# Attention's order of issue made anew in an attention and experts kernel on one core

## The chip, the core and the metric

One core of one Trainium2 chip runs the whole program. The metric is the device time of an execution in microseconds (us). Lower is better. The engines are named as the profile names them: PE (TensorE's matmuls), PEld (its weight loads), DVE (VectorE), ACT (ScalarE), POOL (GpSimd) and SP (SyncE, which issues most of the transfers).

## The reference

Three layers follow each other. The change touches only the first and the first preparation of the second.

```python
# attention: batch 4, 8 heads, 576 positions, 64 per head
scores = scale * np.matmul(q, k.transpose(0, 1, 3, 2))
cum = np.cumsum(np.log(np.clip(f, 0.0001, 1.0)), axis=-1)
scores = np.where(causal, -1000000000.0, scores + cum[:, :, :, None] - cum[:, :, None, :])
attn = np.exp(scores - np.max(scores, axis=-1, keepdims=True))
attn = attn / (np.sum(attn, axis=-1, keepdims=True) + 1e-09)
x = np.matmul(attn, v)            # then laid out as 2304 tokens of 512
# gated layer, widths 512 to 1024 to 512
x = (((x @ w1) * (x @ w2)) @ w3) @ w_out
# experts: each token goes to one of 8, widths 512 to 1024 to 512
y[t] = gate_w[t] * eom[t] * (np.maximum(x[t] @ e1[e], 0) @ e2[e])
```

## The kernel before

**Attention's tiles.** A pair of heads fills the 128 partitions, 64 for each head, so there are 16 pairs (4 batches of 4). The scores are wanted more exactly than one matmul in `fp32r` gives. So q and k are split: the high part is a copy by ACT (`high`, L191, stages `qh` and `kh`), the low part is the rest, by DVE (`low`, L198, `ql` and `kl`). A second set of scores, from the high parts alone, serves to find each row's maximum.

**The stages of a pair.** `lk`, `lq`, `lv` load (L176). `ck` puts the decays into `CK` (L183, L185): for pair 0 from the tile `EK`, for the others from its copy in DRAM, `EKd` (L188). `qd` moves the last 64 queries on the diagonal of `QD` (L171). `X0` to `X3` are the scores for the maxima (L205), and `m0` to `m3` the maxima (L231, two instructions each, one per head). `XL` (L223, L224) and `mL` (L231 on `xl`) do the last 64 rows, which stand alone. `Tm` turns the maxima `M` by a matmul with the identity (L238), `tc` copies them (L241), and `mv` sends them on SP (L171) to `MR`, one row for each head. `GA` to `GD` are the exact scores of four banks (L205, three products each), and `HA` to `HD` add decay and maximum (L205 with `MR` and `CK`). `eA` to `eD` are the exponentials by ACT (L267). `a0` to `a4` cut off the later keys on POOL (L273, "select"), `s1` to `s3` add the blocks on POOL for the row sums (L285). `p0`, `p1`, `p3` multiply with v (L294), `su` sums (L310), `xa` and `sa` copy the results out (L314, L317), and `zs` stores the sums (L321). For each batch, `ri` (L329 to L332) loads its sums, adds 1e-9, inverts them on DVE and stores them to `rz`. `xl` and `xm` (L69, L340), in pairs 7 and 11 alone, load inverses and multiply the first tokens with them on POOL. `cr` clears rows for the experts (L350).

**Weights in between.** `w3` and `w_out` are multiplied with each other once, exactly, before the gated layer uses them. They come as 24 pieces of 64-bit numbers. `Combined.narrow` takes a piece through seven steps: `c0` the load (L430), `c1` ACT (L437), `c2`, `c3`, `c4` on DVE (L439, L441, L443), `c5` ACT (L446) and `c6` POOL (L448). Three buffers hold loaded pieces, and `c4` is the last to read one; four hold the pieces in work. `EARLY` = 12 pieces are done within attention, one in each pair from the third on. The 16 products (`product`, L494 to L496, 12 matmuls each) come after it, the first four of them (`P0` to `P3`) beside the last pair, and the other pieces are converted beside the products.

**What sets the order.** Each engine runs its instructions in the order in which they are issued. Within attention a table sets that order: stage x of pair n has the time `START[x] + PERIOD * n`, all are sorted by it, and they are issued in that order. `AFTER` adds entries behind the last pair. The times in the table are labels to sort by.

```python
order = [(START[x] + SHIFT.get((n, x), 0.0) + PERIOD * n, n, i, x) for n in range(B * NP) for i, x in enumerate(START)]
order = sorted(order + [(t + PERIOD * (B * NP - 1), B * NP, 0, x) for x, t in AFTER.items()])
```

Of the kernel before, what the change touches and what calls it, by code (L numbers as in the profile page):

```python
# [28 lines left out]
P = 128  # L29
# [32 lines left out]
    "inputs": 14.0, "scores": 14.6, "P0": 28.2, "P1": 28.3, "P2": 30.3, "P3": 30.4,  # L62
# [9 lines left out]
def attention(nc, tc, ident, xT, rz, xs, wc, q, k, v, f):  # L72
# [7 lines left out]
    with (  # L80
# [32 lines left out]
        Ms = [p1.tile([P, 32], F32, name=f"M{i}") for i in range(2)]  # L113
# [64 lines left out]
        def decay(s):  # L178
            n = s["n"]
            for h in range(2):  # L180
                dst = CKs[n % 3][64 * h + 1:64 * h + 3, :S]
                if n == 0:
                    move(dst, EK[h:h + NH + 1:NH])  # L183
                else:
                    SP.dma_start(out=dst.bitcast(F32), in_=EKd[:, 2 * n + h, :])  # L185
            if n == 0:
# [50 lines left out]
        def turn(s):  # L237
            PE.matmul(s["x", 4][0:32, 896:1024], Ms[s["n"] % 2], ident, start=True, stop=True)  # L238
# [84 lines left out]
        def invert(s):  # L323

            if s["n"] % NP == NP - 1:
# [3 lines left out]
                SP.dma_start(out=z, in_=view(zd))  # L329
                V.tensor_scalar(out=z, in0=z, scalar1=1e-9, scalar2=None, op0=ALU.add)  # L330
                V.reciprocal(z, z)
                SP.dma_start(out=view(rz), in_=z)  # L332
# [9 lines left out]
        def clear_rows(s):  # L342
# [12 lines left out]
            "zs": (store_sums,), "ri": (invert,), "cr": (clear_rows,), "xl": (first_tile, 0), "xm": (first_tile, 1),  # L355
# [11 lines left out]
        for step in range(7):  # L367
            stages[f"c{step}"] = (lambda s, step: wc.upto(step, min(s["n"] - 1, EARLY)), step)
# [856 lines left out]
```

## Time and profile before

| | |
|---|---|
| time, median of 3 runs | 864.07 us (863.25 to 866.69) |
| the profiled execution's own time | 864.87 us |
| its span, first to last instruction | 863.3 us |
| mean granted clock of TensorE, as a share of full speed | 0.972 |
| PE busy | 804.7 us (93%) |
| DVE busy | 458.8 us (53%) |
| POOL busy | 373.4 us (43%) |
| ACT busy | 280.3 us (32%) |

Attention takes about the first quarter of the span. The shares are means over the whole of it, and over the 40 slices of the page they change much:

```profile
PE   6898898998969889999999999998899999999995
PEld 3666566666747668788788788897778899999983
DVE  6589879780798862333234033044456845446430
ACT  2456456552355441221221221222122122232321
POOL 5477689695365572013023021014255544354421
PEclk7799999899989999999999999999999999999998
DMA  3446675601555311001010010034556564566460
```

Each digit is a slice of 21.6 us (863.3 / 40), in tenths of it, and a 9 is 90% or more. The first ten slices are attention, the next two or three the products of the weights. The last line but one is the clock granted to TensorE. In a timeline row stand the start, the duration, the engine, the line, the operation, out <- in by the program's names and the shapes; in brackets, where the engine had been idle, for how long and what ended that.

### The profile page before, as it was taken

The numbers are of one execution on the slowest core, as the hardware profiler recorded it, in microseconds if no ns is written. First come the engines' busy times: TensorE is split into PE (matmuls) and PEld (weight loads), VectorE is DVE, ScalarE is ACT, GpSimd is POOL, SyncE is SP. The second block draws the span as 40 slices with busy tenths as digits, with TensorE's granted clock in tenths as the row PEclk, the third lists the DMA queues.
The fourth block names the chain that finished last, engine by engine and source line by source line (L and its number), as shares of the span: only waits on it lengthen the run. The fifth ranks groups of instructions, "written<-read, shape, count | busy, mean of one in ns | idle before, by whom it ended". The sixth has DMA issues, their size and how long they took to land.

```text
span 863.3 us, 13769 instructions
## 1 busy us (share of the span) xinstructions
PE 804.7 (93%) x5140; PEld 652.2 (76%) x5140; DVE 458.8 (53%) x950; ACT 280.3 (32%) x536; POOL 373.4 (43%) x383
## 2 busy tenths in 40 slices
PE   6898898998969889999999999998899999999995
PEld 3666566666747668788788788897778899999983
DVE  6589879780798862333234033044456845446430
ACT  2456456552355441221221221222122122232321
POOL 5477689695365572013023021014255544354421
PEclk7799999899989999999999999999999999999998
DMA  3446675601555311001010010034556564566460
GB/s 97 121 132 207 188 226 170 184 22 37 194 170 182 137 49 39 25 38 36 13 50 19 0 44 13 1 106 139 157 149 232 192 207 132 185 204 207 147 254 28
DMA packets 40340, 102.12 MB, mean 118 GB/s; under 512 B 8610, under 2 KB 9314, under 8 KB 40016
## 3 DMA queue, kind: packets, MB, share of 16 engines
q1 hardware_dynamic: 37088, 91.46, 33.5%
q0 software_dynamic: 3184, 9.77, 3.0%
q8 instruction: 41, 0.67, 0.3%
q14 instruction: 27, 0.22, 0.1%
HBM read 84.49 MB, written 16.51 MB: 117 GB/s over the span
## 4 chain that ended last, share of the span: by engine, by line
PE 63%; DVE 14%; DMA 10%; issue 8%; ACT 2%; POOL 1%; SPq 0%; POOLq 0%; DVEq 0%; ACTq 0%
DVE junk L231 4%; PE y L532 4%; PE y L531 4%; PE y L530 4%; DMA xs<-xr,pos 3%; PE h L532 3%; PE h L530 3%; PE h L531 3%; PE a L530 3%; PE a L532 3%; PE b L530 3%; PE a L531 3%; PE b L531 3%; PE b L532 3%; PE v L294 2%
## 5 line engine op out<-in xcount | busy, mean ns | idle before, releaser
L560 DVE TENSOR_TENSOR ga<-b,ga 128x512 f32<-128x512 f32 (+1 forms) x40 | 25.4, 636 | 150.4 <-PE b L532 147.3
L675 POOL DMA_INDIRECT xs<-xr,pos x18 | 19.1, 1062 | 186.0 <-DVE pos L671 130.6
L231 DVE CUSTOM_DVE_ANT_0 junk<-x,tri 128x256 f32<-128x256 f32 (+3 forms) x128 | 62.7, 490 | 9.9 <-PE x L205 0.8
L530 PE MATMUL h<-gh,ah 128*128 128x320 f32 (+4 forms) x224 | 67.2, 300 | 0.0
L531 PE MATMUL h<-gl,ah 128*128 128x320 f32 (+4 forms) x224 | 66.9, 299 | 0.0
L532 PE MATMUL h<-gh,al 128*128 128x320 f32 (+4 forms) x224 | 66.9, 299 | 0.0
L530 PE MATMUL a<-xh,w1h 128*128 128x512 f32 (+1 forms) x160 | 60.9, 381 | 3.2 <-ACT w1h L446 2.2
L532 PE MATMUL a<-xh,w1l 128*128 128x512 f32 (+1 forms) x160 | 60.0, 375 | 3.2 <-POOL w1l L448 3.2
L530 PE MATMUL b<-xh,w2h 128*128 128x512 f32 (+1 forms) x160 | 60.5, 378 | 0.9 <-DVE raw L735 0.9
L273 POOL TENSOR_SCALAR_AFFINE_SELECT PT<-PT 128x256 f32<-128x256 f32 (+1 forms) x80 | 40.3, 522 | 47.4 <-ACT PT L267 47.4
L531 PE MATMUL b<-xl,w2h 128*128 128x512 f32 (+1 forms) x160 | 59.9, 374 | 0.0
L531 PE MATMUL a<-xl,w1h 128*128 128x512 f32 (+1 forms) x160 | 59.9, 374 | 0.0
L532 PE MATMUL b<-xh,w2l 128*128 128x512 f32 (+1 forms) x160 | 59.4, 372 | 0.0
L530 PE MATMUL y<-raw,gh 128*128 128x512 f32 x144 | 57.7, 401 | 1.4 <-ACT gh L561 1.4
L532 PE MATMUL y<-raw,gl 128*128 128x512 f32 x144 | 56.8, 394 | 0.9 <-DVE gl L563 0.9
L531 PE MATMUL y<-raw,gh 128*128 128x512 f32 x144 | 57.0, 396 | 0.0
L523 POOL TENSOR_SCALAR bh<-rb 128x1024 fp32r<-128x1024 f32 x28 | 34.8, 1245 | 48.1 <-DMA rb<-e 40.8
L561 ACT ACTIVATE gh<-ga 128x512 fp32r<-128x512 f32 (+1 forms) x40 | 23.6, 590 | 95.9 <-DVE ga L560 95.9
L951 DVE SCALAR_TENSOR_TENSOR hl<-h,hh 128x320 fp32r<-128x320 f32 (+4 forms) x56 | 25.4, 463 | 50.6 <-ACT hh L950 49.8
L294 PE MATMUL v<-PT,vr 128*64 128x448 f32 (+4 forms) x384 | 49.8, 396 | 1.1 <-ACT zs L317 1.1
L285 POOL TENSOR_TENSOR ac<-ac,PT 128x640 f32<-128x640 f32 (+1 forms) x32 | 44.5, 1390 | 2.6
L524 DVE TENSOR_TENSOR bl<-rb,bh 128x1024 fp32r<-128x1024 f32 x28 | 37.8, 1373 | 14.1 <-POOL bh L523 14.1
(610 smaller groups left out, 2230.0 us busy)
## 6 DMA issues: line engine op xcount, KB each, us to landing
ra<-e SPq DMA_DIRECT2D x28, 512.0 KB
rb<-e SPq DMA_DIRECT2D x28, 512.0 KB
w<-w3t SPq DMA_DIRECT2D x16, 512.0 KB
xs<-zero SPq DMA_DIRECT2D x8, 771.0 KB
vr<-v SPq DMA_DIRECT2D x16, 320.0 KB
kr<-k SPq DMA_DIRECT2D x16, 288.0 KB
qr<-q SPq DMA_DIRECT2D x16, 288.0 KB
wo<-wo SPq DMA_DIRECT2D x8, 512.0 KB
```

The costliest lines, as they stand in the source:

```text
L231: V.tensor_tensor_reduce(out=junk[:, :w], in0=s["x", i][:, 512 * h:512 * h + w] if i < 4 else s["x", i][:, 224:224 + S], in1=tri[:, 640 - ...
L273: G.affine_select(out=t, in_=t, pattern=[[0, 2], [1, w]], compare_op=ALU.is_ge, fill=0.0, base=0, channel_multiplier=-1,)
L285: G.tensor_tensor(out=acc[:, :, q0 - P:], in0=first if j == 1 else acc[:, :, q0 - P:], in1=src, op=ALU.add)
L294: PE.matmul(s["v"][HALF[h], 384 + q0:384 + q1], s["vr"][:, j, HALF[h]], place(s, j, h, q0, q1), start=(j == 0), stop=(j == 4 or q1 == P),)
L523: G.tensor_scalar(out=hi, in0=src, scalar1=1.0, scalar2=1.0, op0=ALU.mult, op1=ALU.mult)
L524: lo_eng.tensor_tensor(out=lo, in0=src, in1=hi.bitcast(F32), op=ALU.subtract)
L530: PE.matmul(ps, ah, bh, start=start and i == 0, stop=False)
L531: PE.matmul(ps, ah, bl, start=False, stop=False)
L532: PE.matmul(ps, al, bh, start=False, stop=stop and i == last)
L560: V.tensor_tensor(out=ga[:, :w], in0=pb[:, :w], in1=ga[:, :w], op=ALU.mult)
L561: A.activation(out=gh[:, f, :w], in_=ga[:, :w], func=ACTF.Copy)
L951: V.scalar_tensor_tensor(out=hl[:, f, :w], in0=ps[:, :w], scalar=0.0, in1=hh[:, f, :w].bitcast(F32), op0=ALU.max, op1=ALU.subtract)
```

## The change

The table `START` has a new time for nearly every stage, so the order of issue changes on every engine. `AFTER` gets ten entries of a new kind: `Kx_y` brings step x of the weights' conversion to y pieces done. With these and with `EARLY + 2` for the first two steps, four pieces more (12 to 15) are through DVE's steps within the last pairs, and loads of more are issued. The inversion of a batch's sums becomes three stages: `rl` the load, `rv` DVE's step, 21.4 later in the table, and `rs` the store. The maxima have 64 instead of 32 columns, and the turn fills 64 partitions. The decays of pairs 0, 1 and 2 come straight from `EK`, and the copy to DRAM is made with pair 2's. The arithmetic is the same.

```diff
 PERIOD = 9.8
 START = {
...
-    "kl": -4.4, "m1": -3.17, "m3": -3.16, "m2": -2.79, "c0": -2.74, "X0": -2.67, "m0": -2.37, "ql": -1.52, "qd": 0.69,
...
+    "kl": 1.21, "XL": 2.1, "mL": 3.54, "Tm": 3.61, "tc": 3.98, "ql": 4.35, "mv": 6.59, "cr": 7.59, "GA": 8.35,
...
 AFTER = {
-    "inputs": 14.0, "scores": 14.6, "P0": 28.2, "P1": 28.3, "P2": 30.3, "P3": 30.4,
+    "K4_13": 3.595, "K0_15": 3.605, "K0_16": 3.615, "K4_14": 3.625, "K0_17": 3.635, "inputs": 11.329, "scores": 13.382,
+    "K1_15": 18.064, "K1_16": 18.074, "K4_15": 18.084, "K0_18": 18.094, "K4_16": 18.104, "P0": 28.286, "P1": 28.296,
+    "P2": 28.306, "P3": 28.316,
 }
...
-        Ms = [p1.tile([P, 32], F32, name=f"M{i}") for i in range(2)]
+        Ms = [p1.tile([P, 64], F32, name=f"M{i}") for i in range(2)]
...
             for h in range(2):
                 dst = CKs[n % 3][64 * h + 1:64 * h + 3, :S]
-                if n == 0:
-                    move(dst, EK[h:h + NH + 1:NH])
+                if n < 3:
+                    move(dst, EK[2 * n + h:2 * n + h + NH + 1:NH])
                 else:
                     SP.dma_start(out=dst.bitcast(F32), in_=EKd[:, 2 * n + h, :])
-            if n == 0:
+            if n == 2:
                 for r in range(2):
                     SP.dma_start(out=EKd[r], in_=EK[NH * r:NH * r + NH].bitcast(F32))
...
         def turn(s):
-            PE.matmul(s["x", 4][0:32, 896:1024], Ms[s["n"] % 2], ident, start=True, stop=True)
+            PE.matmul(s["x", 4][0:64, 896:1024], Ms[s["n"] % 2], ident, start=True, stop=True)
...
-        def invert(s):
+        def invert(s, step):
...
-                SP.dma_start(out=z, in_=view(zd))
-                V.tensor_scalar(out=z, in0=z, scalar1=1e-9, scalar2=None, op0=ALU.add)
-                V.reciprocal(z, z)
-                SP.dma_start(out=view(rz), in_=z)
+                if step == 0:
+                    SP.dma_start(out=z, in_=view(zd))
+                elif step == 1:
+                    V.tensor_scalar(out=z, in0=z, scalar1=1e-9, scalar2=None, op0=ALU.add)
+                    V.reciprocal(z, z)
+                else:
+                    SP.dma_start(out=view(rz), in_=z)
...
-            "zs": (store_sums,), "ri": (invert,), "cr": (clear_rows,), "xl": (first_tile, 0), "xm": (first_tile, 1),
+            "zs": (store_sums,), "rl": (invert, 0), "rv": (invert, 1), "rs": (invert, 2), "cr": (clear_rows,), "xl": (first_tile, 0), "xm": (first_tile, 1),
...
-            stages[f"c{step}"] = (lambda s, step: wc.upto(step, min(s["n"] - 1, EARLY)), step)
+            stages[f"c{step}"] = (lambda s, step: wc.upto(step, min(s["n"] - 1, EARLY + (2 if step < 2 else 0))), step)
...
                 if n == B * NP:
-                    wc.product(*wc.steps.pop(0))
+                    if x[0] == "K":
+                        wc.upto(int(x[1]), int(x[3:]))
+                    else:
+                        wc.product(*wc.steps.pop(0))
                     continue
```

Line numbers of the changed kernel are up to 9 higher: L198 becomes L201, L231 L234, L273 L276, L285 L288, L430 L439, L439 L448, L441 L450, L443 L452, L446 L455 and L448 L457. In the rows that follow, the numbers behind a name tell apart the buffers and pairs (`ql_6` belongs to pair 6); an `ISA` row that gives only `M` is the second half of the maximum above it.

**The middle of attention, DVE.** The rows run from the end of pair 6's queries' low part, or its keys', to pair 7's first maxima. Before:

```order
L198 TENSOR_TENSOR ql_6_1037<-qr_6_796,qh_6_947 128x576
L439 TENSOR_SCALAR w01u_1039<-w01u_1039 128x512
L441 SCALAR_TENSOR_TENSOR w01u_1039<-w01_854,w01u_1039 128x512
L231 ISA junk_125,M0_120<-xl_6_1097,tril_123 128x576
L231 ISA M0_120 128x1
L443 SCALAR_TENSOR_TENSOR wo1u_880<-wo1_700,wo1u_880 128x512
L198 TENSOR_TENSOR kl1_117<-kr_7_939,kh1_115 128x576
L231 ISA junk_125,M1_121<-x1_7_1121,tri_122 128x256
L231 ISA M1_121 128x1
L231 ISA junk_125,M1_121<-x1_7_1121,tri_122 128x256
L231 ISA M1_121 128x1
L231 ISA junk_125,M1_121<-x3_7_1130,tri_122 128x512
```

Now:

```order
L201 TENSOR_TENSOR kl0_116<-kr_6_802,kh0_114 128x576
L448 TENSOR_SCALAR w02u_1084<-w02u_1084 128x512
L450 SCALAR_TENSOR_TENSOR w01u_769<-w01_691,w01u_769 128x512
L234 ISA junk_125,M0_120<-xl_6_1110,tril_123 128x576
L234 ISA M0_120 128x1
L452 SCALAR_TENSOR_TENSOR w01u_769<-w01_691,w01u_769 128x512
L201 TENSOR_TENSOR ql_6_1141<-qr_6_933,qh_6_964 128x576
L234 ISA junk_125,M1_121<-x1_7_1132,tri_122 128x256
L234 ISA M1_121 128x1
L234 ISA junk_125,M1_121<-x1_7_1132,tri_122 128x256
L234 ISA M1_121 128x1
L234 ISA junk_125,M1_121<-x3_7_1145,tri_122 128x512
```

`kl` of the same pair stands where `ql` stood, ahead of the last-rows maximum and behind all eight other maxima. `ql` stands where the next pair's `kl` stood, behind the last step of a piece (L443, now L452).

**The same cycle, POOL.** The rows are the selects and adds of pair 5, whose sum tile is `ac_5`. Before:

```order
L273 AFFINE_SELECT PT_5_1063<-PT_5_1063 128x2x128
L448 TENSOR_TENSOR cw_95<-w00u_726,cw_95 128x512
L273 AFFINE_SELECT PT_5_1063<-PT_5_1063 128x2x128 x2
L273 AFFINE_SELECT PT_5_1063<-PT_5_1063 128x2x64
L285 TENSOR_TENSOR ac_5_1263<-PT_5_1063 128x896
L273 AFFINE_SELECT PT_5_1063<-PT_5_1063 128x2x128
L285 TENSOR_TENSOR ac_5_1263<-ac_5_1263,PT_5_1063 128x2x320
L285 TENSOR_TENSOR ac_5_1263<-ac_5_1263,PT_5_1063 128x2x192
```

Now:

```order
L276 AFFINE_SELECT PT_5_1091<-PT_5_1091 128x2x128
L276 AFFINE_SELECT PT_5_1091<-PT_5_1091 128x2x64
L276 AFFINE_SELECT PT_5_1091<-PT_5_1091 128x2x128 x2
L288 TENSOR_TENSOR ac_5_1226<-PT_5_1091 128x896
L276 AFFINE_SELECT PT_5_1091<-PT_5_1091 128x2x128
L288 TENSOR_TENSOR ac_5_1226<-ac_5_1226,PT_5_1091 128x2x320
L457 TENSOR_TENSOR cw_95<-w01u_769,cw_95 128x512
L288 TENSOR_TENSOR ac_5_1226<-ac_5_1226,PT_5_1091 128x2x192
```

Two selects (the 128 and the 64 wide one) move ahead, and the piece's step (L448, now L457) moves from among the selects to the place between the second and the third add.

**The last pair, DVE.** The rows run from the last-rows maximum of pair 15 to the inversions. Before:

```order
L198 TENSOR_TENSOR ql_15_2455<-qr_15_2225,qh_15_2371 128x576
L231 ISA junk_125,M1_121<-xl_15_2509,tril_123 128x576
L231 ISA M1_121 128x1
L443 SCALAR_TENSOR_TENSOR w13u_2308<-w13_2128,w13u_2308 128x512
L330 TENSOR_SCALAR z_11_2531<-z_11_2531 128x36
L331 RECIPROCAL z_11_2531<-z_11_2531 128x36
L330 TENSOR_SCALAR z_15_2747<-z_15_2747 128x36
L331 RECIPROCAL z_15_2747<-z_15_2747 128x36
L439 TENSOR_SCALAR wo4u_2813<-wo4u_2813 128x512
L441 SCALAR_TENSOR_TENSOR wo4u_2813<-wo4_2805,wo4u_2813 128x512
```

Now:

```order
L234 ISA junk_125,M1_121<-xl_15_2527,tril_123 128x576
L234 ISA M1_121 128x1
L448 TENSOR_SCALAR wo4u_2192<-wo4u_2192 128x512
L450 SCALAR_TENSOR_TENSOR wo4u_2192<-wo4_2112,wo4u_2192 128x512
L452 SCALAR_TENSOR_TENSOR wo4u_2192<-wo4_2112,wo4u_2192 128x512
L448 TENSOR_SCALAR w04u_2353<-w04u_2353 128x512
L450 SCALAR_TENSOR_TENSOR w04u_2353<-w04_2269,w04u_2353 128x512
L452 SCALAR_TENSOR_TENSOR w04u_2353<-w04_2269,w04u_2353 128x512
L201 TENSOR_TENSOR ql_15_2556<-qr_15_2358,qh_15_2388 128x576
L448 TENSOR_SCALAR w14u_2683<-w14u_2683 128x512
```

Six steps of the pieces `wo4` and `w04` (the thirteenth and fourteenth) now stand between the last-rows maximum and `ql_15`; the inversions follow after two more pieces.

**The last pair, SP.** The rows run from the inversion's load to the transfer of pair 15's maxima (`MR1`). Before:

```order
L171 DMA QD1_119<-qh_15_2371 64x64 x2
L329 DMA z_11_2531<-zd_106 128x1x36
L332 DMA rz_63<-z_11_2531 8x16x36
L176 DMA vr_14_2553<-v 128x640
L171 DMA MR1_111<-mt_15_2525 2x4x128
L171 DMA MR1_111<-mt_15_2525 2x1x64
L321 DMA zd_106<-zs_12_2476 2x2x288
```

Now:

```order
L333 DMA z_11_2443<-zd_106 128x1x36
L174 DMA QD1_119<-qh_15_2388 64x64 x2
L324 DMA zd_106<-zs_12_2495 2x2x288
L439 DMA w14_2544<-w3t 128x512
L439 DMA wo5_2547<-wo 128x512
L439 DMA w05_2552<-w3t 128x512
L179 DMA vr_14_2562<-v 128x640
L174 DMA MR1_111<-mt_15_2554 2x4x128
L174 DMA MR1_111<-mt_15_2554 2x1x64
```

Three loads of pieces now stand ahead of v's load and of the maxima's transfer. The third piece (`w05`) needs a buffer that `w04` has been in.

**The start, SP.** The rows are the first issues of transfers. Before:

```order
L99 DMA fc_102<-f 32x576
L176 DMA kr_0_202<-k 128x576
L176 DMA qr_0_204<-q 128x576
L171 DMA CK0_107<-EK_104 2x576 x2
L188 DMA EKd_105<-EK_104 32x576 x2
L176 DMA kr_1_211<-k 128x576
L176 DMA qr_1_215<-q 128x576
L185 DMA CK1_108<-EKd_105 2x576 x2
L171 DMA QD0_118<-qh_0_213 64x64 x2
```

Now:

```order
L102 DMA fc_102<-f 32x576
L179 DMA kr_0_202<-k 128x576
L179 DMA qr_0_204<-q 128x576
L174 DMA CK0_107<-EK_104 2x576 x2
L179 DMA kr_1_209<-k 128x576
L174 DMA QD0_118<-qh_0_211 64x64 x2
L179 DMA qr_1_243<-q 128x576
L174 DMA CK1_108<-EK_104 2x576 x2
L179 DMA kr_2_254<-k 128x576
```

The last queries' transfer (`QD0`) moves ahead of the second pair's queries, and the copies to DRAM and back (`EKd`) are gone from here.

## Rows read from the trace of the kernel before

**Rows 1.** Table of stages: us, busy us of PE, PEld, DVE, ACT, POOL; PEclk, DMA, GB/s.

```profile
46.03:186.42 140.39, 128.46 (x1322) 91.67 (x1322) 120.45 (x280) 80.09 (x131) 110.29 (x111) 0.95 0.56 171
186.40:208.10 21.70, 19.50 (x226) 13.78 (x224) 4.52 (x14) 9.89 (x16) 18.94 (x21) 1.00 0.13 35
230.00:264.40 34.40, 25.42 (x97) 18.68 (x95) 32.79 (x33) 16.35 (x29) 23.70 (x15) 0.90 0.50 163
```

**Rows 2.** PE timeline, first matmuls of gA: start, us, what, idle before.

```profile
79.66 0.36 PE L205 MATMUL gA<-qh,kh 64*128 64x192 f32 x2 [0.85 <-DVE M L231]
...
127.93 0.36 PE L205 MATMUL gA<-qh,kh 64*128 64x192 f32 x2 [0.22 <-DVE M L231]
...
138.48 0.30 PE L205 MATMUL gA<-qh,kh 64*128 64x192 f32 x2
```

**Rows 3.** DVE timeline behind the last-rows maximum in two passes.

```profile
73.85 2.49 DVE L443 SCALAR_TENSOR_TENSOR w00u<-w,w00u 128x512 int32<-128x512 int32 x1
76.27 0.95 DVE L198 TENSOR_TENSOR kl<-kr,kh 128x576 fp32r<-128x576 f32 x1
...
84.53 0.75 DVE L231 CUSTOM_DVE_ANT_0 junk<-xl,tril 128x576 f32<-128x576 f32 x1
```

**Rows 4.** POOL timeline, first and second adds and the selects ahead.

```profile
73.69 2.10 POOL L285 TENSOR_TENSOR ac<-PT 128x896 f32<-128x896 f32 x1
...
84.06 1.43 POOL L273 TENSOR_SCALAR_AFFINE_SELECT PT<-PT 128x256 f32<-128x256 f32 x3
...
88.96 1.55 POOL L285 TENSOR_TENSOR ac<-ac,PT 128x640 f32<-128x640 f32 x1
...
136.32 2.10 POOL L285 TENSOR_TENSOR ac<-PT 128x896 f32<-128x896 f32 x1
```

**Rows 5.** SP's queue, issues, at the inversion and at the products' first load.

```profile
99.88 0.65 SPq L332 DMA_DIRECT2D rz<-z  x1
...
101.08 0.42 SPq L430 DMA_DIRECT2D wo<-wo  x1
...
214.35 0.45 SPq L430 DMA_DIRECT2D wo<-wo  x1
```

**Rows 6.** PE timeline, where it waited for transfers.

```profile
14.78 0.58 PE L223 MATMUL xl<-kh,QD 128*128 128x288 f32 x1 [3.40 <-DMA QD<-qh]
...
105.24 0.82 PE L205 MATMUL gA<-MR,CK 64*128 64x192 f32 x4 [1.35 <-DMA MR<-mt]
...
197.00 0.51 PE L205 MATMUL gA<-MR,CK 64*128 64x192 f32 x4 [1.10 <-DMA MR<-mt]
```

**Rows 7.** The table of stages, gA's HA to the last queries in two passes.

```profile
80.50:83.54 3.04, 2.97 (x40) 2.51 (x37) 2.83 (x9) 2.21 (x3) 1.47 (x2) 1.00 0.73 220
105.24:110.46 5.22, 5.20 (x37) 4.78 (x37) 1.39 (x3) 2.78 (x4) 1.73 (x3) 0.50 0.89 228
```

**Rows 8.** ACT timeline, a first exponential and the products' first conversion.

```profile
81.03 0.97 ACT L267 ACTIVATE PT<-gA 128x960 f32<-128x960 f32 x1 [1.59 <-PE gA L205]
...
218.55 0.66 ACT L437 ACTIVATE wo4u<-wo 128x512 f32<-128x512 f32 x1 [9.35 <-DMA wo<-wo]
```

**Rows 9.** DVE timeline, pieces of weights beside the products.

```profile
219.31 0.43 DVE L439 TENSOR_SCALAR wo4u<-wo4u 128x512 int32<-128x512 int32 x1 [5.64 <-ACT wo4u L437]
...
232.68 0.68 DVE L443 SCALAR_TENSOR_TENSOR w05u<-w,w05u 128x512 int32<-128x512 int32 x1
233.29 1.78 DVE L441 SCALAR_TENSOR_TENSOR w15u<-w,w15u 128x512 int32<-128x512 int32 x1
```

**Rows 10.** POOL timeline, last step of piece 23.

```profile
259.17 1.73 POOL L448 TENSOR_TENSOR raw<-w17u,raw 128x512 fp32r<-128x512 f32 x1
```

**Rows 11.** PE timeline, one pair of products, and a wait for a piece.

```profile
219.14 0.39 PE L494 MATMUL wc<-cw,raw 128*128 128x512 f32 x1
...
224.58 0.39 PE L494 MATMUL wc<-raw,raw 128*128 128x512 f32 x1
...
257.56 0.80 PE L496 MATMUL wc<-raw,raw 128*128 128x512 f32 x1 [3.05 <-POOL raw L448]
```

13 rows, old and new, of the table START are left out of this document.

## The prediction

> **Words.** Attention works on 16 pairs of heads. I call the stretch from pair n's first gA matmul to pair n+1's the pass of n. Per pass VectorE (DVE) does eight maxima (L231), the last-rows maximum, kl and ql (L198) and, for a weight piece, L439, L441 and L443. GpSimd (POOL) does five selects (L273), three adds (L285, "first add" the long one) and L448.
>
> **What bounds the kernel now.** I read the table of stages first. From 46.03 to 186.42 there are twelve passes in 140.4 us, 11.7 each; PE is busy 128.5 of it and DVE 120.5 [rows 1]. Then the first matmuls of gA: at 79.66 they had waited 0.85 for a maximum; the pass from 127.93 took 10.55 and ended without a wait [rows 2]. So PE needs about 10.5, and DVE hands it the buffers late. Why, the DVE and POOL timelines show: L443 took 2.49 and began 0.16 after POOL's first add, which ran 73.69 to 75.79; it ended at 76.34, 0.55 after the add [rows 3, 4]. In the pass that took 10.55 the first add came only 8.39 in (136.32), behind that work [rows 4]. A second loss is the inversion: SP's store of the inverse stood at 99.88 ahead of the maxima's transfer, and PE waited 1.35 for it at 105.24 [rows 5, 6]; after that the same work took 5.22 at a granted clock of 0.50 (1.2 GHz) where it had taken 3.04 at 1.00 (2.4 GHz) [rows 7]. The last pair pays the same again, 1.10 at 197.00 [rows 6]. Last, from 230.00 to 264.40 PE is busy 25.4 of 34.4, and DVE 32.8 [rows 1]: the products wait for pieces of weights.
>
> **The change, part by part.** Four stretches of the span, each before and after.
>
> *Start, to gA of pair 2 (46.03).* The transfer of the last queries moves ahead of the decays' trip through DRAM and of the second pair's queries. PE waited 3.40 for it at 14.78 [rows 6]. What is late next is DVE, which is busy with the maxima of pairs 0 and 1; they come earlier by the two kl that move from ahead of them to behind them (up to 0.95 each, 76.27 [rows 3]). Bounds 0 and 3.4; I take 2, what DVE leaves. In the two passes that follow, ql stands where kl stood and is held by the first add likewise, but the add comes some 0.5 earlier (next part): 0.5 each. **-3.0.** The decays' three pairs of copies without DRAM and 64 instead of 32 columns of maxima are in this, at nothing: the turn's moving side keeps 128 columns.
>
> *Twelve middle passes.* DVE's order after the last-rows maximum was L443, kl, maxima; now L443, ql, maxima, and kl runs after the eight maxima, where L448 no longer falls on L441. POOL's selects a4 and a0 move ahead of the wait for the third exponential, so only one of the three (1.43 together at 84.06, 4.40 into its pass) is left between it and the first add [rows 4]: the add starts at 4.40 + 0.45 = 4.85, ends at 6.95. The last-rows maximum starts 4.87 in [rows 3] and ends at 5.6, so L443 still runs into the add. From the add's end it goes as in the pass that ended at 79.66: there L443 and kl were done 1.43 after it (75.79 to 77.22), gA came 2.44 later [rows 2, 3]. 6.95 + 1.43 + 2.44 = **10.8 a pass**. The divisors' inversion is now a load, a DVE step 2 pairs and more later and a store, none of which waits: their two disturbed passes go. What is late next: c0's load is issued when L443 frees a buffer (7.5 in) and ACT's L437 wants it one pass later just ahead of the first exponential. One issued at 214.35 was there at 218.55, 4.2 later [rows 5, 8]: that makes 11.7, 0.9 into the next pass, and with L437's 0.66 the exponential could start 1.56 in. It started 1.37 in at 81.03 after a wait of 1.59 for PE [rows 8], so 0.2 is lost where nothing but ACT counts: covered, barely. The products with the divisors (L340, pairs 7 and 11) now stand between POOL's selects; I put 1.0 on both together, between 0 and 3. Twelve passes: 129.6 + 1.0 = 130.6, **-9.8**; bounds 10.5 and 11.4 a pass.
>
> *The last two pairs (186.42 to 208.1, 21.7).* Here the change adds a wait. Two pieces' L439, L441, L443 stand on DVE ahead of ql of pair 15, and on SP the load of the fifth piece begun (w05) stands ahead of the maxima's transfer; it waits for the buffer that the second of them frees. DVE from 5.6 on meets the first add until 6.95, then a select (0.4), the second add (1.55 at 88.96 [rows 4]) and the third (1.0 by its size). When both want to go on they alternate: L441 took 1.78 at 233.29, right behind an L443 that took 0.68 and freed DVE after 0.61 (232.68 [rows 9]); I read the rest of the 1.78 as an operation of POOL that went in between. By turns, with 0.4 for L439 (219.31 [rows 9]) and 0.6 for L441 and L443: 7.35, select 7.75, 8.35, add 9.9, 10.5, add 11.5, then 11.9, 12.5, 13.1. From there, a load, v's load and the transfer: at 101.08 such a load was issued and PE got the maxima at 105.24, 4.16 later [rows 5, 6]. So HA of pair 15 starts 17.3 into the stretch instead of 10.58 (197.00): +6.7. PE idles some 7 us, so its clock falls: +2.2 [rows 7]. Two L437 of 0.66 [rows 8] now stand ahead of the copy that frees v for pair 15: +1.3. **+10.2**, bounds +5 (DVE goes first each time, w05 at 10.15, and PE holds its clock) and +13.
>
> *The products (208.1 to 264.4, 56.3).* Two took 5.44 (219.14 to 224.58), so sixteen need 43.5 [rows 11]. PE waited up to 3.05 for a piece (257.56) [rows 11]. DVE started on piece 12 at 219.31 [rows 9], and piece 23 was done on POOL at 260.90 [rows 10]: 41.6 for twelve. Now 12 to 15 lack ACT's and POOL's step alone and 16's load is there; DVE starts on piece 16 as soon as the last inverse is done, 6.2 in at the latest (SP issued the load behind its store at 214.35 [rows 5]). Eight pieces at that pace need 27.7, so 23 is done 34 to 38 in, wanted at 41. PE does not wait: 43.7, **-12.6**; bounds -9 and -13.5. After it everything shifts: the gated stage's order is the same.
>
> **Sum:** -3.0 - 9.8 + 10.2 - 12.6 = -15.2. The profiled execution took 864.87 (span 863.3) and so becomes 849.7. It stood 0.80 above the median of the runs, 864.07, so I forecast **848.9**.
>
> **A rule weighed.** L443 and the first add show that one waits for all of the other [rows 3, 4], and kl behind them took only 0.95 at 76.27: it went ahead of the second add [rows 3]. The Trainium skill, SBUF — State Buffer, section "Who interferes with whom", says that a VectorE operation with two SBUF inputs and a GpSimd operation that reads SBUF lock each other out for the whole instruction, and that the order of issue decides who blocks. That speaks against this order, which leaves L443 and ql where POOL adds; taken at its worst, with POOL issuing first both times, it gives the third rival's pass. The trace agrees with the lock, and so far not with POOL winning twice.
>
> **Rivals.** (1) *The first add is late as before*: a load that lands late holds ACT's exponentials by 0.7, L443 goes first and ql then waits for the whole add, as before. Twelve at 11.4 plus 1.0: -2.6 instead of -9.8, 856.1. For it: the load has no margin. Against: a pass with L443 unhindered issues the next load earlier. Chance 0.17. (2) *POOL falls behind and stays out of the way*, as in the passes of 10.55, and in the last pairs DVE goes first (w05 at 10.15, +7.2): -3.0 - 12.8 + 7.2 - 12.6 = -21.2, 842.9. Chance 0.17. (3) *Slower: the second add slips in ahead of ql in every pass.* 1.55 more, 12.35 a pass and 149.2 for twelve, +8.8, so 867.5; and where the idle then drops the clock, 2.2 more for each such pass, with six of them 881. It decides from 12.1 a pass on. Against: 0.95 at 76.27. Chance 0.09. (4) *The begun pieces buy nothing*, loads and not DVE pacing the products: -2.6, 861.5. Against: DVE's 32.8 of 34.4. Chance 0.07. My forecast, 843 to 855 by itself, has 0.50.
>
> **How the numbers follow.** A measurement of this kernel can tell about 0.5%, 4.3 us, from no change. Faster by more: the forecast and rivals 1 and 2, 0.84; within: rival 4, 0.07; slower: rival 3, 0.09. The range 838 to 861 takes in rivals 1, 2 and the bounds of the terms, and leaves out rival 3 and part of 4.
>
> **What would show it.** In the changed profile: twelve passes near 10.8 without a low clock in the middle; the last queries' matmuls before 12.5; gA of pair 2 near 43. At the last pair PE idle for ql and then for the transfer of the maxima, HA some 17 into the stretch, clock at 1.2 GHz behind it. PE without a wait of over 0.3 from product 1 to 16, their sum near 44. Wrong would be: passes of over 11.2, a PE wait on L446 or L448 among the products, or no gap at pair 15.

## The result and the profile after

The changed kernel takes 857.15 us (median of 6 runs, 855.28 to 859.01) against 864.09 of the kernel before: a ratio of 0.9916, with a 95% interval of 0.9897 to 0.9935. That is 6.9 us, not the 15.2 of the forecast. The profiled execution took 857.55 with a span of 855.9; that of before took 864.87.

The table of stages of the changed kernel, with the columns of [rows 1], has the middle passes (gA of pair 2 to gA of pair 14), the last two pairs and the products:

```profile
44.66:179.94 135.28, 123.10 (x1324) 88.71 (x1322) 113.19 (x278) 82.08 (x134) 112.91 (x113) 0.99 0.59 183
179.94:213.25 33.31, 24.21 (x222) 17.98 (x222) 15.19 (x26) 9.86 (x15) 15.54 (x18) 0.80 0.26 85
213.25:257.10 43.85, 43.85 (x197) 36.16 (x194) 36.48 (x40) 22.28 (x39) 27.63 (x18) 1.00 0.45 145
```

The four stretches, each against its forecast (start: to gA of pair 2):

| stretch | before | after | change | forecast |
|---|---|---|---|---|
| start | 46.03 | 44.66 | -1.4 | -3.0 |
| twelve middle passes | 140.4 | 135.3 | -5.1 | -9.8 |
| last two pairs | 21.7 | 33.3 | +11.6 | +10.2 |
| products | 56.3 | 43.85 | -12.4 | -12.6 |
| sum | | | -7.3 | -15.2 |

What follows the products starts 7.3 earlier and ends 7.4 earlier, so these stretches hold the whole difference. The products came as forecast; the middle lacks 4.7, the start 1.6, the last pairs 1.4.

**An undisturbed pass** reads as forecast. PE, gA of pairs 12 and 13 (10.87 apart; six of the twelve passes take 10.83 to 10.87, three 10.46 to 11.05), to be read beside [rows 2]:

```profile
156.57 0.36 PE L208 MATMUL gA<-qh,kh 64*128 64x192 f32 x2 [0.62 <-DVE M L234]
...
167.44 0.36 PE L208 MATMUL gA<-qh,kh 64*128 64x192 f32 x2 [0.65 <-DVE M L234]
```

In between, on DVE the piece's last step (L452, L443 before) and ql, beside [rows 3]:

```profile
161.97 2.16 DVE L452 SCALAR_TENSOR_TENSOR w12u<-w,w12u 128x512 int32<-128x512 int32 x1
164.05 0.95 DVE L201 TENSOR_TENSOR ql<-qr,qh 128x576 fp32r<-128x576 f32 x1
```

and on POOL the first and the second add, beside [rows 4]:

```profile
161.48 2.11 POOL L288 TENSOR_TENSOR ac<-PT 128x896 f32<-128x896 f32 x1
...
164.48 1.93 POOL L288 TENSOR_TENSOR ac<-ac,PT 128x640 f32<-128x640 f32 x1
```

The first add starts 4.91 into the pass (forecast 4.85). L452 meets it and ends 0.54 after it; ql goes ahead of the second add, and gA comes 2.44 behind ql's end.

**One pass goes as rival 1 has it.** Pass 3, from gA at 55.12, takes 11.63. The load of a piece (issued at 51.83) lands late: ACT's conversion of it starts 5.3 behind its issue, where 4.2 was forecast. So the conversion (L446, L437 before) and the exponentials behind it are late, and the first add starts 6.08 into the pass (at 61.20, for 2.48). L452 goes ahead of it, and ql waits for the whole add:

```profile
57.15 0.68 ACT L446 ACTIVATE w01u<-w 128x512 f32<-128x512 f32 x1 [2.02 <-DMA w<-w3t]
```

```profile
61.64 2.66 DVE L201 TENSOR_TENSOR ql<-qr,qh 128x576 fp32r<-128x576 f32 x1
```

**Two passes are long**, those of pairs 9 and 13. PE's timeline, gA of pairs 9, 10 and 14, and the matmuls of the last queries (L226, L223 before) in either pass:

```profile
121.19 0.36 PE L208 MATMUL gA<-qh,kh 64*128 64x192 f32 x2 [0.83 <-DVE M L234]
...
127.74 0.58 PE L226 MATMUL xl<-kh,QD 128*128 128x288 f32 x1 [2.60 <-DMA QD<-qh]
...
135.28 0.30 PE L208 MATMUL gA<-qh,kh 64*128 64x192 f32 x2
...
172.64 0.37 PE L226 MATMUL xl<-kh,QD 128*128 128x288 f32 x1 [1.25 <-DMA QD<-qh]
...
179.94 0.36 PE L208 MATMUL gA<-qh,kh 64*128 64x192 f32 x2 [0.99 <-DVE M L234]
```

The passes take 14.09 and 12.50 (from 167.44, above), 4.9 over two of 10.84. PE waited 2.60 and 1.25 for `QD`, the transfer of the last queries. SP's queue ahead of that transfer in the first of them:

```profile
117.90 0.33 SPq L439 DMA_DIRECT2D w<-w3t  x1
118.33 1.15 SPq L174 DMA_DIRECT2D MR<-mt  x2
119.60 2.41 SPq L72 DMA_DIRECT2D rb<-rz  x4
122.39 0.40 SPq L356 DMA_DIRECT2D xs<-zero  x1
122.86 1.99 SPq L174 DMA_DIRECT2D QD<-qh  x2
```

Behind the maxima's transfer stand four loads of inverses (`rb<-rz` x4, 2.41 of issuing), and `QD` is issued 1.67 after gA. In the pass of 10.87 from 156.57 it was issued 1.67 ahead of gA, at 154.90. The granted clock of the pass of 14.09 is 0.88.

**The last pair** is as forecast, a little worse. On DVE the first conversion step and, six steps later, ql of pair 15; on SP the fifth load and the maxima's transfer; on PE the waits, beside [rows 6]:

```profile
185.34 1.86 DVE L448 TENSOR_SCALAR wo4u<-wo4u 128x512 int32<-128x512 int32 x1
...
192.46 0.75 DVE L201 TENSOR_TENSOR ql<-qr,qh 128x576 fp32r<-128x576 f32 x1
```

```profile
192.57 0.33 SPq L439 DMA_DIRECT2D w<-w3t  x1
...
193.47 1.15 SPq L174 DMA_DIRECT2D MR<-mt  x2
```

```profile
193.27 0.53 PE L208 MATMUL gA<-ql,kh 64*128 64x192 f32 x2 [4.47 <-DVE ql L201]
...
196.93 0.82 PE L208 MATMUL gA<-MR,CK 64*128 64x192 f32 x4 [2.35 <-DMA MR<-mt]
...
208.05 0.81 PE L297 MATMUL v<-PT,vr 128*64 128x128 f32 x6 [2.20 <-ACT zs L320]
```

PE waits 4.47 for ql, 2.35 for MR, and 2.20 for the copy of pair 14's sums, which stands on ACT behind two steps of pieces; that last wait was 1.10 before. HA starts 17.0 into the stretch, and the granted clock is 0.80 over it, where [rows 1] has 1.00.

### The profile page after: what moved, and what is told of

Same layout as the page of the kernel before. It is cut to its first block, busy times and chain, and to the rows that moved or that the text cites. A ratio compares the mean times of both kernels' runs of the same rounds, so it can differ in the third digit from the quotient of the medians.

```text
span 855.9 us, 13772 instructions
## 1 busy us (share of the span) xinstructions
PE 800.8 (94%) x5140; PEld 654.6 (76%) x5140; DVE 453.7 (53%) x950; ACT 280.7 (33%) x536; POOL 373.6 (44%) x383
## 4 chain that ended last, share of the span: by engine, by line
PE 63%; DVE 16%; DMA 9%; issue 7%; ACT 2%; SPq 1%; POOL 0%; POOLq 0%; DVEq 0%; ACTq 0%
DVE junk L234 5%; PE y L541 4%; PE y L539 4%; PE y L540 4%; PE h L541 3%; PE h L539 3%; PE h L540 3%; DMA xs<-xr,pos 3%; PE a L539 3%; PE b L539 3%; PE a L541 3%; PE a L540 3%; PE b L540 3%; PE b L541 3%; PE q L539 2%
## 5 line engine op out<-in xcount | busy, mean ns | idle before, releaser
L684 POOL DMA_INDIRECT xs<-xr,pos x18 | 18.9, 1050 | 187.9 <-DVE pos L680 130.6
L234 DVE CUSTOM_DVE_ANT_0 junk<-x,tri 128x256 f32<-128x256 f32 (+3 forms) x128 | 62.7, 489 | 10.4 <-PE x L208 1.3
L276 POOL TENSOR_SCALAR_AFFINE_SELECT PT<-PT 128x256 f32<-128x256 f32 (+1 forms) x80 | 42.6, 545 | 48.5 <-ACT PT L270 48.1
L297 PE MATMUL v<-PT,vr 128*64 128x448 f32 (+4 forms) x384 | 52.4, 412 | 2.2 <-ACT zs L320 2.2
L288 POOL TENSOR_TENSOR ac<-ac,PT 128x640 f32<-128x640 f32 (+1 forms) x32 | 45.5, 1421 | 1.6
```

Of the source, the lines that this page charges most:

```text
L234: V.tensor_tensor_reduce(out=junk[:, :w], in0=s["x", i][:, 512 * h:512 * h + w] if i < 4 else s["x", i][:, 224:224 + S], in1=tri[:, 640 - ...
L276: G.affine_select(out=t, in_=t, pattern=[[0, 2], [1, w]], compare_op=ALU.is_ge, fill=0.0, base=0, channel_multiplier=-1,)
L288: G.tensor_tensor(out=acc[:, :, q0 - P:], in0=first if j == 1 else acc[:, :, q0 - P:], in1=src, op=ALU.add)
L297: PE.matmul(s["v"][HALF[h], 384 + q0:384 + q1], s["vr"][:, j, HALF[h]], place(s, j, h, q0, q1), start=(j == 0), stop=(j == 4 or q1 == P),)
```

## The experiments

Theory after this comparison: the forecast's mechanisms hold, and the missing gain lies (a) on SP, where the loads of inverses hold the last queries, and (b) in the last pair, where the begun pieces stand ahead of ql and of the maxima. The rivals are that POOL's products make the long passes, and that the conversion work is merely paid in one place or the other. Ratios are against the kernel before in the same comparison. Medians are given with the number of runs.

### Without the pieces begun

```diff
-    "K4_13": 3.595, "K0_15": 3.605, "K0_16": 3.615, "K4_14": 3.625, "K0_17": 3.635, "inputs": 11.329, "scores": 13.382,
-    "K1_15": 18.064, "K1_16": 18.074, "K4_15": 18.084, "K0_18": 18.094, "K4_16": 18.104, "P0": 28.286, "P1": 28.296,
+    "inputs": 11.329, "scores": 13.382, "P0": 28.286, "P1": 28.296,
...
-            stages[f"c{step}"] = (lambda s, step: wc.upto(step, min(s["n"] - 1, EARLY + (2 if step < 2 else 0))), step)
+            stages[f"c{step}"] = (lambda s, step: wc.upto(step, min(s["n"] - 1, EARLY)), step)
```

> The changed kernel without the four pieces begun (no K entries, no EARLY + 2); all else as changed. Theory: the begun pieces took 11.6 in the last two pairs (33.3 from pair 14's gA to the first product, against 21.7 before) and gave back 12.4 in the products (43.9 against 56.3). So the last two pairs fall to 22 to 24, gA's HA of pair 15 starts 10.5 to 11.5 into them, the products rise to 55 to 57 with PE waits on L455 and L457, and the time is 857 to 860, about that of the change. Rival (the loads, and not DVE's steps, paced the products): the products stay near 44 and the time falls to 846.

853.18 us (4 runs), ratio 0.9886 (0.9830 to 0.9942): by the times not told apart from the change, though the median is 4 under what was expected. In its profile the last two pairs take 19.9 instead of 33.3, the products 55.5 instead of 43.85, and the middle 132.8 instead of 135.3; the last product ends 4.5 earlier (252.6). The last two pairs come out 2 under the 22 expected at least. The products do not stay near 44, so the rival falls. So the pieces gave 11.65 in the products, as forecast, and cost 13.4 at the last pair and 2.4 in the middle. The 2.4 was in no expectation. It is pass 13, 10.06 here. SP's queue there, in this run and then in the changed kernel:

```profile
162.63 1.14 SPq L173 DMA_DIRECT2D MR<-mt  x2
163.87 2.40 SPq L71 DMA_DIRECT2D rb<-rz  x4
166.32 1.23 SPq L173 DMA_DIRECT2D QD<-qh  x2
```

```profile
164.16 0.33 SPq L439 DMA_DIRECT2D w<-w3t  x1
164.59 1.15 SPq L174 DMA_DIRECT2D MR<-mt  x2
165.84 2.40 SPq L72 DMA_DIRECT2D rb<-rz  x4
168.29 1.23 SPq L174 DMA_DIRECT2D QD<-qh  x2
```

The same four loads of inverses, but the load of a piece (`w04`) ahead of them is gone. In the changed kernel it was issued at 164.16, when the L452 that frees its buffer had ended (164.13), and held what stands behind it. Here `QD` is issued 0.8 ahead of gA (167.13) and there 0.85 after it, and PE has no wait.

### The pieces begun behind the last pair's ql and maxima

```diff
-    "K4_13": 3.595, "K0_15": 3.605, "K0_16": 3.615, "K4_14": 3.625, "K0_17": 3.635, ...
+    "K4_13": 8.2, "K0_15": 8.21, "K0_16": 8.22, "K4_14": 8.23, "K0_17": 15.6, ...
```

> The changed kernel with the begun pieces' DVE steps and loads issued behind the last queries' low part and behind the maxima's transfer of pair 15, the fifth load behind v's load. Theory (ql of pair 15 behind six steps, and the transfer behind a load that waits for the second of them, cost 6.8 of PE's time and then the clock): HA of pair 15 starts 10.5 to 12 into the stretch instead of 17.0, the first product comes 6 to 9 earlier, the products stay within 1 of 43.9, and the time is 849 to 852. Rival (the conversion work is only pushed into the products, which then wait for pieces): products 48 or more, time 855 to 857.

842.11 us (4 runs), ratio 0.9759 (0.9718 to 0.9800): 15 us under the change, more than expected. The table of stages, last two pairs and products:

```profile
178.54:199.89 21.35, 19.08 (x223) 14.30 (x223) 15.47 (x23) 9.65 (x15) 17.15 (x18) 1.00 0.33 107
199.89:243.69 43.80, 43.80 (x197) 36.15 (x193) 35.12 (x41) 20.36 (x36) 26.78 (x18) 1.00 0.45 147
```

The last two pairs fall from 33.3 to 21.35 with the clock at 1.00, and the products stay at 43.8: the same pieces, and of the 13.4 that they cost at the last pair 12.0 are gone. The other 1.4 (21.35 against 19.9 without the pieces) stay: PE still waits 2.20 for the sums' copy, which stands on ACT behind two steps of pieces, where it waits 1.10 without them. The rival falls. HA of pair 15 starts 9.2 into the stretch. The steps on DVE and the loads on SP were moved together, so this run does not tell them apart. (The profiled execution is 15.2 shorter: 12.0 of it here, 0.8 at the start, 0.6 in the middle, and 1.8 after the products, where nothing was changed and executions differ by as much, see below.)

### The first tiles one at a time

```diff
-            for i in {7: (0, 1), 11: (2, 3)}.get(s["n"], ()):
+            for i in {7: (0,), 8: (1,), 11: (2,), 12: (3,)}.get(s["n"], ()):
```

> The changed kernel with the four first tiles' loads of inverses and products taken one at a time, in pairs 7, 8, 11 and 12 instead of two in pair 7 and two in pair 11. Theory (the two issues more of SP ahead of the last queries' transfer, and the second 1.5 of POOL ahead of the first add, make the passes of 14.1 and 12.5 long): the four passes concerned take 10.9 to 11.9 each, together 3 to 4 less than the 46.4 that passes 9, 10, 13 and the first of the last stretch's length take now; time 853 to 855. Rival (POOL's 3 us are lost wherever they stand): two passes at 12.4, the sum as now, time 857.

854.81 us (5 runs), ratio 0.9892 (0.9854 to 0.9930). The middle takes 132.8, 2.5 less. But passes 9 and 10 take 11.86 and 12.16, and PE still waits for `QD` in both, 1.22 and 2.06. Two issues in each of two passes cost 2.3 over passes of 10.84, where four in one cost 3.3. The four passes concerned take 43.66 together, against 45.45 in the change (the expectation has 46.4): 1.8 less, not 3 to 4, though the time is as expected. The run halved both suspects at once and so did not tell them apart.

### The loads of inverses a pass earlier

```diff
-    ... "xl": 27.09, ... "rv": 57.6, "rs": 63.34, ...
+    ... "xl": 21.1, ... "rv": 47.8, "rs": 53.54, ...
```

> The changed kernel with SP's four loads of inverses (L72) issued most of a pass earlier, behind the next pair's queries and decays instead of ahead of the last queries' transfer (the inverse's two later steps come one pass earlier for it); POOL's products stay where they are. Theory A (SP's 2.4 us of issues hold the last queries' transfer): PE's waits of 2.60 and 1.25 for QD go; if that decides, pass 9 falls from 14.1 to 12 and pass 13 from 12.5 to 11.8, and the time to 854.5. Theory B (POOL's products alone hold the first add): the waits for QD go, the passes stay within 0.3, and the time is 857.

846.90 us (4 runs), ratio 0.9807 (0.9766 to 0.9849). The middle takes 130.0 (forecast for the change: 130.6). The table of stages, middle passes; then in pass 9 SP's issues, PE's last queries and POOL's products and first add:

```profile
43.77:173.77 130.00, 121.43 (x1324) 87.71 (x1324) 113.64 (x279) 80.75 (x133) 111.18 (x112) 1.00 0.61 190
```

```profile
111.75 2.39 SPq L72 DMA_DIRECT2D rb<-rz  x4
...
119.45 1.94 SPq L174 DMA_DIRECT2D QD<-qh  x2
```

```profile
124.33 0.37 PE L226 MATMUL xl<-kh,QD 128*128 128x288 f32 x1
```

```profile
123.61 2.96 POOL L346 TENSOR_TENSOR xT<-xT,rb 128x512 f32<-128x512 f32 x2
...
128.59 2.10 POOL L288 TENSOR_TENSOR ac<-PT 128x896 f32<-128x896 f32 x1
```

`QD` is issued 0.88 ahead of gA (120.33), and PE has no wait. POOL's products still take 2.96 at the same place, and the pass takes 10.16, less than an undisturbed one. Pass 13 takes 10.07. So theory A holds and B falls. The passes gained more than A forecast (12 and 11.8), and the time lies 7.6 under its 854.5: of the 8.4 that the profiled execution gained, 5.3 lie in the middle, 0.9 at the start, and 1.9 in the last two pairs, where PE waits 0.87 for MR instead of 2.35.

The edit moves the inverse's step on DVE and its store as well, and that was not run alone. In the changed kernel the store ahead of pass 9 was issued at 114.38, and SP had issued all behind it by 115.52 and then stood until the piece's load at 117.90, so the store did not hold `QD`. It is settled that the loads' place in the queue decides; whether by the time of issuing alone or also by the bytes they move at that moment was not separated.

### The inversion in one piece

```diff
-    ... "rl": 36.24, "rv": 57.6, "rs": 63.34, ...
+    ... "rl": 44.2, "rv": 44.2001, "rs": 44.2002, ...
```

> The changed kernel with the inversion in one piece again (load, DVE's step and store behind each other, at the time that the table had before). Theory A (the split freed the two disturbed passes): SP's store waits for DVE ahead of the maxima's transfer, PE waits 1 to 1.5 for MR and its clock falls; two more passes of 12 to 14, the middle 139 to 142, time 862 to 865. Theory B (it was the four loads of inverses ahead of the last queries' transfer that made those passes long, before and after, and the split gave little): the middle 135 to 137, time 857 to 859.

870.19 us (10 runs), ratio 1.0058 (1.0034 to 1.0083): 13 us over the change, more than either theory said. In the profiled execution, the longest of the ten (874.22), passes 7 and 11 become 16.0 and 16.4, the middle 146.8 at a granted clock of 0.94, and the last pair waits 6.08 for MR. PE at pair 7's maxima:

```profile
103.85 0.82 PE L208 MATMUL gA<-MR,CK 64*128 64x192 f32 x4 [3.02 <-DMA MR<-mt]
```

Before, that wait was 1.35 [rows 6]. In this order of issue the split is worth 13 us.

### The selects a4 and a0 behind the third exponential's

```diff
-    ... "a4": 12.13, ... "a0": 16.76, ...
+    ... "a4": 17.2, ... "a0": 17.3, ...
```

> The changed kernel with the selects a4 and a0 behind the third exponential's select a1 again. Theory (their move lets the first add begin 4.9 instead of 5.7 us into the pass, and all behind it follows the add): the undisturbed passes take 11.3 to 11.6 instead of 10.84, the middle 139 to 143, time 862 to 866. Rival (the add's start does not decide): 10.84 as now, time 857.

862.39 us (10 runs), ratio 0.9994 (0.9972 to 1.0015). Seven passes take 11.34 to 11.36, with waits of PE for a maximum such as

```profile
99.85 0.35 PE L208 MATMUL gA<-qh,kh 64*128 64x192 f32 x2 [1.09 <-DVE M L234]
```

In that pass POOL's first add starts 5.38 in (at 105.23), not 4.9, with 5.7 forecast. As expected, half a microsecond of a pass comes from the first add's earlier start. The time is 5.2 over the change. The profiled execution was the shortest of the ten (860.44); its middle took 138.0, 1 under what was expected and only 2.8 over the change, since pass 3 was 10.06 here and 11.63 there.

### kl and ql in each other's places

```diff
-    ... "kl": 1.21, ... "ql": 4.35, ...
+    ... "kl": -5.45, ... "ql": 1.21, ...
```

> The changed kernel with kl and ql in each other's places on DVE, as before (ql ahead of the last-rows maximum, the next pair's kl behind the piece's last step). Theory (each takes 0.75 to 0.95 in either place): undisturbed passes 10.7 to 11.0; at the last pair PE has ql at once but waits for MR until 16 to 17 into the stretch all the same, since the transfer stands behind the fifth load; at the start pair 0's gA comes up to 0.7 later; time 856 to 859. Rival (the swap carries the gain of the middle, since the low part that stands behind the add is now the one that gA needs last): passes of 11.3 or more, time over 861.

857.81 us (5 runs), ratio 0.9915 (0.9887 to 0.9943): no difference. Undisturbed passes take 10.81 to 10.89. At the last pair ql is there at once, and PE waits 7.63 for MR instead of 4.47 and 2.35: HA starts 17.0 into the stretch as before. The swap by itself gives nothing, and of the last pair's two waits the transfer's is the one that ends last.

### Small parts

Pair 0's kl behind its last-rows maximum (`SHIFT = {(0, "kl"): 2.4}`):

> The changed kernel with pair 0's kl issued behind its last-rows maximum. Theory (kl held that maximum by 0.67 on DVE, and so the turn, the next pair's scores and gA): PE's turn (L241) starts at 15.2 instead of 15.88 and pair 0's gA at 19.2 to 19.4 instead of 19.89. Rival (pair 1's queries or decays come no earlier): 19.8 to 20.0.

One run, 855.98 us. The turn starts at 15.47 and gA at 19.49 instead of 19.89: 0.4, a little less than expected.

The decays of pairs 1 and 2 through DRAM (`if n == 0:` at both places):

> The changed kernel with the decays of pairs 1 and 2 by way of DRAM again, the copy being made with pair 0's. Theory (these transfers lie beside DVE's maxima, with 2 us to spare): pair 0's gA at 19.9 to 20.3. Rival (the trip holds pair 1's first scores): 20.9 or later.

One run, 856.15 us. gA starts at 19.90, where the change has 19.89. The decays without DRAM give nothing there. (Pair 2's gA comes at 43.71; in the other runs it lies between 43.66 and 44.86.)

Maxima of 32 columns:

> The changed kernel with maxima of 32 columns and a turn of 32. Theory (the moving side has 128 columns either way): no pass differs by more than 0.1 from 10.84, time 856 to 858.5. Rival (the wider turn costs in each of 16 passes): the time differs by 1.5 or more.

855.14 us (5 runs), ratio 0.9899 (0.9861 to 0.9936), 2 less than the change and 0.9 under what was expected, with intervals that overlap. Three passes take 10.84 to 10.89, but passes 5 to 7 take 11.12, 10.69 and 10.72, more than the 0.1 that was allowed, and pass 9 takes 15.8, with a wait of 3.01 for `QD` and a granted clock of 0.78. Why it is longer than the 14.1 of the change was not looked for. No cost or gain of the wider turn is shown.

### Both moves together

```diff
+    ... "xl": 21.1, ... "rv": 47.8, "rs": 53.54, ...
...
+    "K4_13": 8.2, "K0_15": 8.21, "K0_16": 8.22, "K4_14": 8.23, "K0_17": 15.6, ...
+    "K1_15": 18.464, "K1_16": 18.474, "K4_15": 18.484, "K0_18": 18.494, "K4_16": 18.504, ...
```

> The begun pieces behind the last pair's maxima's transfer (as in the run that moved them) and SP's loads of inverses a pass earlier (as in that run), and the two ACT steps that stood ahead of the copy of the sums (L320) moved behind it. Theory (two independent losses of 12 and 5, and one of 1.1): middle 130, last two pairs 19.5 to 21, products 43.9, the last product ends at 237 to 240 and the time is 835 to 838. Rival (the passes, once shorter, run into DVE or the loads): middle over 132 or products over 46, time 840 or more.

842.62 us (6 runs, 836.11 to 843.93), ratio 0.9745 (0.9714 to 0.9776). The median lies 4.6 over what was expected, two of the six runs within it. The profiled execution is the shortest of the six (836.11), so what lengthened the others does not show. In it the middle and the products are what the theory gives, 129.97 and 43.8; the last two pairs take 22.3, since a new wait came up:

```profile
192.35 0.81 PE L297 MATMUL v<-PT,vr 128*64 128x128 f32 x6 [3.47 <-DMA vr<-v]
```

v's load of pair 15 stood on SP behind the inverse's store of the third batch, and that waited for DVE behind the begun pieces. The run with this mended and pair 0's kl moved:

```diff
+SHIFT = {(0, "kl"): 2.4, (11, "rv"): 9.8, (11, "rs"): 9.8}
```

> As e10_both, with two things more: the inverse's last two steps of the third batch a pass later, so that v's load of pair 15 no longer stands behind a store that waits for DVE, and pair 0's kl behind its last-rows maximum. Theory: PE's wait of 3.47 for v goes, the last two pairs take 18.5 to 19.5 and pair 0's gA starts at 19.2 to 19.4; the last product ends at 235 to 237, 3 to 4.5 earlier than in e10_both, and the time is 3 to 5 below that run's 842.6. Rival (what waits at the end of attention is only met again in the products): the products take 46 or more, time 841 to 843.

838.67 us (6 runs, 834.79 to 842.09), ratio 0.9702 (0.9669 to 0.9735), 18 us under the change and 25 under the kernel before. The wait for v is gone, but PE waits 1.10 for the sums' copy and 1.91 for POOL's last add, and the last two pairs still take 21.9; the last product ends at 240.2, not at 235 to 237. What was won there was met again: of the expectation the mechanism came (the wait for v) and not the gain. The two versions are not told apart; both beat the change clearly.

## Why the prediction was right and wrong

- **What bounds the kernel: right.** DVE hands PE the buffers late because L443 runs into POOL's first add. Undisturbed passes took 10.84 (10.8 was forecast), and with the selects moved back 11.35 (11.4 was rival 1's pass). The Trainium skill, SBUF — State Buffer, section "Who interferes with whom", has an exclusive lock between the two engines. The trace agrees: L452 began 0.49 after the add and took 2.16, and it took 0.69 where POOL was idle (210.55). That POOL wins twice, as in the third rival, was seen in no undisturbed pass.
- **Twelve middle passes: wrong by 4.7**, and this is the step that failed: "The products with the divisors (L340, pairs 7 and 11) now stand between POOL's selects; I put 1.0 on both together, between 0 and 3." The two passes cost 4.9. Place and mechanism were wrong too: POOL's products cost nothing (10.16 with them, once SP's queue was free), and the four loads that serve them stood on SP ahead of the last queries. I priced the instructions of the moved stage on POOL and did not follow its transfers past those behind them in SP's queue. In pass 9 (3.3 of the 4.9) the four loads were enough. In pass 13 (1.7) it took them and the load of a begun piece ahead of them, which waited for its buffer: without either one that pass took 10.1. The forecast had such a load hold a transfer at the last pair alone. The other passes lack some 0.7, as pass 3 went as in rival 1.

  The kernel before had the same four loads ahead of the last queries, in its pass 7 with a transfer issued 4.2 after gA (102.90), and yet no wait of PE for it:

```profile
103.29 3.18 SPq L69 DMA_DIRECT2D rb<-rz  x4
...
107.12 1.14 SPq L171 DMA_DIRECT2D QD<-qh  x2
```

```profile
110.46 0.58 PE L223 MATMUL xl<-kh,QD 128*128 128x288 f32 x1
```

  The wait for the maxima and the low clock behind it [rows 6, 7] had made PE later than the transfer. So the trace of before could not show what the loads cost: the inversion's loss covered it. In the new order they stand two passes later, in a pass of their own.
- **The inversion: right that it goes**, but for more than I said. Whole, in the new order, it costs 13 us, not the two passes' few microseconds.
- **The last two pairs: right in mechanism**, +11.6 for +10.2. HA stood 17.0 into the stretch (17.3 was forecast). The sums' copy behind two L437 made PE wait 2.20 where it had waited 1.10, so 1.1 more (1.3 was forecast). What was sized too small is the clock. Behind HA, PE was busy 4.1 longer than before with as many instructions, at 0.73 instead of 1.00 (2.2 was forecast). The table of stages, HA to the first product, now and before:

```profile
196.93:213.25 16.32, 14.12 (x116) 10.10 (x116) 4.38 (x8) 5.40 (x8) 6.45 (x8) 0.73 0.14 47
```

```profile
197.00:208.12 11.12, 10.02 (x116) 7.00 (x116) 0.00 (x0) 4.09 (x6) 8.62 (x10) 1.00 0.11 33
```

- **The products: right**, 43.85 for 43.7. PE was busy 43.85 of 43.85; the loads did not pace them, and rival 4 falls.
- **The start: -1.4 for -3.0.** The last queries' matmuls came at 12.45, as forecast, but the turn only 1.2 earlier. The kl moved from ahead of pair 0's maxima gave nothing there: the first of them began at 9.91 instead of 9.99, as DVE now waited for PE's scores. And pair 0's last-rows maximum still stood behind its kl on DVE, 0.4 of which was shown. The two passes that follow gave 0.3 and not 1.0. Their first adds did come earlier, by 0.37 and 0.49, but in the second pass PE had no wait to give back, now and before:

```profile
31.89:44.66 12.77, 12.77 (x112) 10.06 (x112) 7.75 (x23) 4.85 (x8) 7.53 (x9) 0.74 0.36 117
```

```profile
33.37:46.03 12.66, 12.66 (x110) 9.82 (x111) 7.66 (x20) 5.42 (x9) 6.92 (x9) 0.76 0.35 114
```

  In the other runs these two passes took 23.8 to 25.0 together (24.8 here, 25.0 before), so the 0.7 that they lack lies within what executions differ by.
- **The rivals.** 857.15 lies beside rival 1's 856.1, but by chance. Rival 1's mechanism, a load that lands late, came in one pass of the twelve, pass 3; in the undisturbed passes the first add was early.

## What to carry to other kernels

When a stage moves, list its transfers too, and read for each what is queued behind it and when that is wanted: four small loads ahead of one needed transfer cost 3.3 us in one pass, 1.7 in another where a load that waited for its buffer stood ahead of them, and nothing a pass earlier. Work begun early pays only if it stands behind what the last stage waits for: ahead of the last low part and the maxima's transfer the same four pieces cost more than the 11.7 that they gave, and behind them 1.4. And a loss may need two causes together, so that taking away either one takes away all of it, or be covered by a larger one in the same pass until the two are parted.

## What was not expected of the hardware

- A pass with 2.96 more of POOL's work took 10.16, and one without it 10.85. The work delays the first add to 8.26 into the pass (128.59), when DVE is done with L452 (1.30 at 125.82, the end of the products within it) and ql (0.84 at 127.04); neither waits for the add. It is the pass of 10.55 of [rows 2, 4] again.
- After the last product, where the order is the same, profiled executions took from 594.6 (both moves together) to 600.5 us (the inversion in one piece), 598.8 with the change. That is as much as some parts of the change, so parts of a few microseconds were read from their own stretch and not from the time of the whole.
